# A dummy operand written by ScalarE, and half of one batch's transposes moved from TensorE to the DMA crossbar

## The chip, the cores and the metric

The kernel runs on one core of a Trainium2 chip. A core has TensorE (PE, matmuls), VectorE (DVE), ScalarE (ACT), GpSimd (POOL) and SyncE (SP), which here only issues DMAs; ScalarE can issue DMAs too. Each of these engines executes its instructions in the order in which the kernel writes them, and waits where an operand isn't there yet. 16 DMA engines move the data. The metric is device time in microseconds. The page gives the profiled execution's span, which is what its times are counted in.

## The reference

Two blocks, one after the other. The first is an attention without a square score matrix (8 batches, 8 heads, 576 positions, 64 per head); the second is a gated feed-forward block over all 4608 positions.

```
q_s = exp(q - max);  q_s = q_s / sum(q_s, over the 64 of a head)
k_s = exp(k - max);  k_s = k_s / sum(k_s, over the 576 positions)
kv  = einsum('bhsd,bhse->bhde', k_s, v)        # 64 x 64 per head
x   = einsum('bhsd,bhde->bhse', q_s, kv)       # -> 4608 x 512
g, val = x @ w_gate, x @ w_val                 # 512 -> 1536
out = (gelu(g) * val) @ w_out                  # 1536 -> 512
```

Input and output are float32; the kernel's matmuls take float16.

## The kernel before, in words

**Tiles.** The 576 positions of a batch lie over 128 partitions: a position is a multiple of nine plus n, and partition pairs hold the nine. Each partition has five columns n of 512 values (8 heads of 64). Column 0 is padding on the even partitions (for k -1e30, whose exp is 0) and the real remainder on the odd ones; columns 1 to 4 are the main part, 4 x 128 = 512 positions. The 64 remaining positions of all eight batches are gathered in one tile, `xtr`, and go through the feed-forward block as a ninth batch (`order` puts it before the last).

**Attention of a batch.** `exp` (L158, ScalarE) writes `eq` and `ek`, two buffers each, used by even and odd batches. `norm_sum` (L176, L178) sums a pair of heads on VectorE and takes the reciprocal; `norm_mul` (L195) multiplies `eq` by it, on VectorE or GpSimd. `cast_v` makes `v` float16. `unit_kv` (L222) multiplies k and v on TensorE for two pairs of heads, and `kv_norm` (L230, L233) scales and masks the result on VectorE into `kv_sb`. For the product with q, `eq` has to be transposed. Three ways are in use: `unit_t` (L305) does eight 128x128 transposes on TensorE for two pairs and copies them from PSUM (batches 0 and 1); `unit_td` (L323) has the DMA crossbar transpose a whole batch, 20 blocks, issued by SP (batches 2 to 7); `unit_trem` (L316) does that for column 0 alone (batches 0 and 1). `xq` and `xqr` pick the tile that a product reads. `unit_x` (L347) is the product of one pair, 128x512, and its copy into `xt`; `unit_xrem` (L363) is that of the remainder.

**Feed-forward of a batch.** For each of 12 blocks of 128 hidden columns, `ffn_fi` does four matmuls psg and four psv (L402); `gate` then has ScalarE take the gelu of psg (L407) and VectorE multiply it by psv (L409) into `ht`. Then for each of four columns n, 12 matmuls psy (L477) make the output rows, which VectorE or ScalarE copies from PSUM (`evac`, L524, L526) and SP stores (L487).

**Order.** The kernel is scheduled by hand. `plan` holds work that rides along: `at(b, kind, i, ...)` puts functions behind block i of batch b's feed-forward (FI) or behind column i of its output (NS; 10 + n or 14 + n lie in the middle of column n). Batch 1's attention rides on batch 0's last block (FI 11: its exps, the norms of pairs 0 to 2) and on its output columns: behind column 1 (NS 5) the transposes of pairs 0 and 1, in column 2 (NS 16) the kv of pairs 0 and 1 and the norm of pair 3, in column 3 (NS 17) the x of pairs 0 and 1. The rest of it lies in `first1`, which `ffn_first` calls between the first three blocks of batch 1: the transposes and kv of pairs 2 and 3 behind block 0, the x of pair 2 behind block 1, that of pair 3 behind block 2. `cut` says after how many of a column's 12 matmuls the middle lies.

**Start.** `warm_pe` runs dummy matmuls (L394) on a tile `warm` of zeros, before the first real work is there. VectorE writes `warm` after it has copied one value of q's first load (L548, L549), so the dummies begin when that load has landed. ScalarE's `preload` makes a one-element activation, to have its table loaded.

**PSUM.** `ps_big` has six banks, taken in turn under the tag "mm": batch 0's four psy, then x of pairs 0 and 1 of batch 1, then batch 1's psg and psv from the first psy's bank on. `ps_att` has two, for the attention's products.

Of the kernel before, what the change touches and what calls it, by code (L numbers as in the profile page):

```python
# [10 lines left out]
f16 = mybir.dt.float16  # L11
# [7 lines left out]
def kernel(  # L19
# [10 lines left out]
    nc = tc.nc  # L30

    B, H, S, D = q.shape
    C = H * D
    F = moe_w_gate.shape[1]
    P = 128
    HP = H // 2
    NFI = F // P
# [3 lines left out]
    NT = S // 64  # L41
    NM = 4
    NC = NM + 1
# [10 lines left out]
    att = ctx.enter_context(tc.tile_pool(name="att", bufs=2))  # L54
# [9 lines left out]
    warm = const.tile([P, 512], f16)  # L64
    ident = const.tile([P, P], f16)
    mask = const.tile([P, 2, D], f32)
    ones = const.tile([P, 1], f16)
    tiny = const.tile([P, 72], f32)
    ek_b, eq_b, v16_b = [], [], []
    for i in range(2):  # L70
# [4 lines left out]
    q0r = const.tile([64, H, D], f32)  # L75
    eq0r = const.tile([P, C], f16)
    ld_b = {nm: [const.tile([P, H, NC * D], f32, name=f"{nm}t{i}") for i in range(n)]
            for nm, n in (("k", 2), ("v", 1), ("q", 2))}
# [22 lines left out]
    QUAD = 2  # L101

    def heads(x, b, h0, h1):

        if b >= QUAD:
            return x.rearrange("p (t c) x -> p c t x", t=2)[:, h0 // 2:h1 // 2]
        return x[:, h0:h1]
# [24 lines left out]
    def copy_on(eng, dst, src):  # L132
        if eng == "pool":
            nc.gpsimd.tensor_copy(out=dst, in_=src)  # L134
        elif eng == "act":
            nc.scalar.copy(out=dst, in_=src)  # L136
        else:
            nc.vector.tensor_copy(out=dst, in_=src)  # L138
# [12 lines left out]
        copy_on(eng, wo_sb[:, 2 * c:2 * c + 2, :], wst[("wo", c)])  # L151


    def exp(nm, b, h0=0, h1=H, n0=0):
        dst = (ek_b if nm == "k" else eq_b)[b % 2]
        o, i = (("p n (c t d) -> p c t n d", "p c t (n d) -> p c t n d") if b >= QUAD else
                ("p n (h d) -> p h n d", "p h (n d) -> p h n d"))
        nc.scalar.activation(  # L158
            out=dst[:, n0:NC, h0 * D:h1 * D].rearrange(o, d=D, **({"t": 2} if b >= QUAD else {})),
            in_=heads(tiles[(nm, b)], b, h0, h1)[..., n0 * D:NC * D].rearrange(i, d=D),  # L160
            func=ACTF.Exp)

# [8 lines left out]

    def norm_sum(b, hp, n0=0):
        n = NC - n0
        e = eq_b[b % 2][:, n0:NC, hp * P:(hp + 1) * P].rearrange("p n (h d) -> p n h d", d=D)
        rq = att.tile([P, n, 2], f32, name="rq", tag="rq", bufs=4)
        nc.vector.reduce_sum(rq, e, axis=mybir.AxisListType.X)  # L176
        rrq = att.tile([P, n, 2], f32, name="rrq", tag="rrq", bufs=4)
        nc.vector.reciprocal(out=rrq, in_=rq)  # L178
        st[(b, "norm", hp)] = (e, rrq, n)

    def norm_pair(b, g, n0, engs):

        n = NC - n0
        e = eq_b[b % 2][:, n0:NC, 2 * g * P:(2 * g + 2) * P].rearrange("p n (h d) -> p n h d", d=D)
        rq = att.tile([P, n, 4], f32, name="rq2", tag="rq2", bufs=2)
        nc.vector.reduce_sum(rq, e, axis=mybir.AxisListType.X)
        rrq = att.tile([P, n, 4], f32, name="rrq2", tag="rrq2", bufs=2)
        nc.vector.reciprocal(out=rrq, in_=rq)
        for j, eng in enumerate(engs):
            st[(b, "norm", 2 * g + j)] = (e[:, :, 2 * j:2 * j + 2], rrq[:, :, 2 * j:2 * j + 2], n)  # L190
            norm_mul(b, 2 * g + j, eng)
# [23 lines left out]
    st = {}  # L215
# [74 lines left out]
    def get_eqt(b):  # L290
        if (b, "eqt") not in st:
            st[(b, "eqt")] = att.tile([P, NC * C], f16, name="eqt", tag="eqt")[
                :, 0:HP * MAIN].rearrange("p (h t) -> p h t", h=HP)
        return st[(b, "eqt")]

    def unit_t(b, g, eng="dve", between=()):
        eqt = get_eqt(b)
        pst = ps_att.tile([P, 2, MAIN], f16, name="pst", tag="att")
        st["evac_t"] = lambda eng: copy_on(eng, eqt[:, 2 * g:2 * g + 2, 0:MAIN], pst)
        for j in range(2):  # L300
            hp = 2 * g + j
            for f in between if j == 1 else ():
                f()
            for n in range(NM):
                nc.tensor.transpose(  # L305
                    pst[:, j, n * P:(n + 1) * P],
                    eq_b[b % 2][:, n + 1, hp * P:(hp + 1) * P], ident)
        if eng:
            st["evac_t"](eng)

    def unit_trem(b):

        src = eq0r[0:64] if b == 0 else eq_b[b % 2][:, 0, :]
        n = src.shape[0]
        t = att.tile([P, HP, n], f16, name=f"eqtr{b}", tag=f"eqtr{b}", bufs=1)
        nc.sync.dma_start_transpose(out=t, in_=src)  # L316
        st[(b, "eqtr")] = t[:, :, 0:n:n // REM]


    def unit_td(b):  # L320
# [3 lines left out]
                                    in_=eq_b[b % 2].rearrange("p n c -> p (n c)"))  # L324
        st[(b, "eqt4")] = t

    def xq(b, hp):

        if (b, "eqt4") in st:
            return st[(b, "eqt4")][:, 1:NC, hp]  # L330
        return st[(b, "eqt")][:, hp, 0:MAIN]

    def xqr(b, hp):
        if (b, "eqt4") in st:
            return st[(b, "eqt4")][:, 0, hp, 0:P:2]
        return st[(b, "eqtr")][:, hp, :]

    def get_xt(b):
# [52 lines left out]
    def warm_pe(n):  # L391
        ps = pswarm
        for _ in range(n):
            nc.tensor.matmul(ps, ident, warm, start=True, stop=True)  # L394

    def preload(func):
        nc.scalar.activation(out=tiny[:, 0:1], in_=tiny[:, 0:1], func=func)
# [146 lines left out]
    def load_batch(b, what=((q, "q"), (k, "k"), (v, "v"))):  # L544
        for src, nm in what:
            load(src, nm, b, 0, H, 0)

    nc.vector.tensor_copy(out=tiny[0:1, 1:2], in_=ld_b["q"][0][0:1, 0, D:D + 1])  # L548
    nc.vector.memset(warm, 0.0)  # L549
    preload(ACTF.Exp)  # L550
    exp("q", 0, 0, 4, 1)
    exp("q", 0, 4, 8, 1)
    exp("k", 0, 0, 4)
    exp("k", 0, 4, 8)
    norm_pair(0, 0, 1, ("dve", "pool"))
    warm_pe(13)
    unit_t(0, 0, None)
    evac_t0 = st["evac_t"]
    norm_pair(0, 1, 1, ("dve", "pool"))
# [20 lines left out]
        load(k, "k", 1, h0, h0 + 4, 0)  # L580
        load(v, "v", 1, h0, h0 + 4, 0)
    load_batch(2, ((q, "q"), (k, "k")))
    for h0 in (0, 4):
        nc.sync.dma_start(out=q0r[:, h0:h0 + 4], in_=q[0, h0:h0 + 4].rearrange(
            "h (m n) d -> m h (n d)", n=NT)[:, :, 0:D])
    cast_w("wg", 0, "pool")
    cast_w("wv", 0, "pool")
    for c in range(1, NW):
# [6 lines left out]
    FI, NS = 0, 1  # L595
    plan = {}

    def at(b, kind, i, *fns):
        plan.setdefault((b, kind, i), []).extend(fns)

    L = lambda f, *a: (lambda: f(*a))

    at(0, FI, NFI - 1, L(exp, "q", 1, 0, 4), L(exp, "q", 1, 4, 8), L(exp, "k", 1, 0, 4),
       L(cast_w_o, 3), L(cast_w_o, 4), L(cast_w_o, 5),
       L(norm, 1, 0), L(norm, 1, 1), L(norm_sum, 1, 2), L(norm_mul, 1, 2, "pool"),
       L(cast_v, 1, 0, 4, "act"), L(exp, "k", 1, 4, 8))
    at(0, NS, 5, L(unit_t, 1, 0))
    at(0, NS, 16, L(unit_kv, 1, 0), L(cast_v, 1, 4, 8), L(load_batch, 2, ((v, "v"),)),
       L(norm, 1, 3))
    at(0, NS, 17, L(unit_x, 1, 0, "act", True), L(unit_x, 1, 1, "act", True))  # L610
    at(0, NS, 7, L(preload, ACTF.Gelu))
    first1 = [[L(unit_t, 1, 1), L(unit_kv, 1, 1)], [L(unit_x, 1, 2, "act")],
              [L(unit_x, 1, 3, "dve")]]

    def x_upper0():
# [20 lines left out]
    for b in range(2, B):  # L636
# [3 lines left out]
        if b + 1 < B:  # L640
            n = b + 1
# [15 lines left out]
    for b in order:  # L657
        xt = get_xt(b) if b < B else xtr
        hts = []
        fi0 = 0  # L660
        if b < 2:
            hts = ffn_first0(xt, (x_upper0, L(unit_x, 0, 3, "dve"))) if b == 0 else ffn_first(xt, first1)
            fi0 = len(hts)
            ride(b, FI, fi0 - 1)
        for fi in range(fi0, NFI):
            hts.append(ffn_fi(xt, fi, b == 1 and fi == 7))
            ride(b, FI, fi)
        if b == 0:
            psys = []
            for ns in range(4):  # L670
                psys.append(ps_big.tile([P, C], f32, name="psy", tag="mm"))
                mm_out(psys[ns], hts, ns, range(0, NFI // 2))
                ride(b, NS, ns)
            for ns in range(4):
                cut = 9 if ns == 2 else 7 if ns == 3 else NFI
                mm_out(psys[ns], hts, ns, range(NFI // 2, cut))
                ride(b, NS, 14 + ns)
                mm_out(psys[ns], hts, ns, range(cut, NFI))
                evac(b, ns, psys[ns], "act" if ns == 3 else "dve")
                ride(b, NS, 4 + ns)  # L680
        else:
            for ns in range(4):
                if b == order[-1] and ns == 3:
                    last_rows(b, hts, ns)
                    break
                psy = ps_big.tile([P, C], f32, name="psy", tag="mm")
                mm_out(psy, hts, ns, range(NFI // 2))
                ride(b, NS, 10 + ns)
                mm_out(psy, hts, ns, range(NFI // 2, NFI))
                evac(b, ns, psy)  # L690
                ride(b, NS, ns)
# [30 lines left out]
```

## Time and profile before

| What | us |
| --- | --- |
| Median of 3 runs (lowest to highest) | 314.37 (314.08 to 315.01) |
| The profiled execution, its own time | 313.89 |
| Its span | 311.9 |
| TensorE matmuls busy | 301.3 |
| VectorE busy | 168.5 |
| ScalarE busy | 139.2 |
| GpSimd busy | 54.0 |
| First dummy matmul starts | 7.00 |
| Batch 1's first psg starts | 48.93 |
| Moved by DMA, and mean rate | 51.61 MB, 165 GB/s |

The page gives busy time by engine, then 40 slices of the span, where a digit is the busy share in tenths. The chain that ended last is followed back from the last instruction through what released each step; it dates a matmul by its place in the pipeline, some 0.15 us later than the timeline's start. In the timeline, a row is start, length, engine, line, operation and tiles; in square brackets stands the idle time before it and what ended it. SPq and ACTq are DMA issues of SP and ScalarE; PEld is TensorE's weight load. Matmuls overlap: a 128x512 one lasts 0.38 us and the next begins 0.216 us after it.

### The profile page before, as it was taken

What the parts mean: (1) busy time and instruction counts of PE and PEld (TensorE: products, weight loads), DVE (VectorE), ACT (ScalarE), POOL (GpSimd) and SP (SyncE); (2) the same over time, 40 slices, a digit from 0 to 9 for tenths busy, and PEclk for the clock granted to TensorE, in tenths of its full rate; (3) what the DMA queues carried; (4) which work ended last, traced back from release to release, by engine and by line L of the source; (5) the groups of instructions that cost most, each with busy time, mean ns of one, the idle gap of its engine ahead of it and who ended that gap; (6) DMA issues with size and microseconds to landing.
All of it is one profiled execution on the core that took longest, in us unless ns stands there. A gap on an engine that the chain in (4) does not pass through costs nothing.

```text
span 311.9 us, 4662 instructions
## 1 busy us (share of the span) xinstructions
PE 301.3 (97%) x1800; PEld 140.1 (45%) x1800; DVE 168.5 (54%) x293; ACT 139.2 (45%) x180; POOL 54.0 (17%) x67
## 2 busy tenths in 40 slices
PE   1999999999999999999999999999999999999995
PEld 0544455444445444444444444444444444444444
DVE  3944386484586478437853686358633443324331
ACT  3663475994843753366235643474330333013300
POOL 2657451071084000110003000300000000000000
PEclk9999999999999999999999999999999999999999
DMA  7999999609999017901593149412210200140002
GB/s 227 372 383 393 402 386 388 181 0 250 378 340 249 0 69 261 338 16 69 185 354 70 67 127 387 93 40 97 52 35 34 103 0 0 35 102 0 0 36 101
DMA packets 55189, 51.61 MB, mean 165 GB/s; under 512 B 18560, under 2 KB 50688, under 8 KB 55168
## 3 DMA queue, kind: packets, MB, share of 16 engines
q1 hardware_dynamic: 53440, 49.68, 49.2%
q10 hardware_dynamic: 1728, 1.64, 1.7%
q8 instruction: 14, 0.23, 0.3%
q14 instruction: 7, 0.06, 0.1%
HBM read 37.75 MB, written 9.44 MB: 151 GB/s over the span
## 4 chain that ended last, share of the span: by engine, by line
PE 96%; DMA 2%; DVE 1%; issue 0%; ACT 0%
PE psg L402 30%; PE psv L402 30%; PE psy L477 29%; DMA qt<-in_q_dram 2%; PE pswarm L394 2%; PE pskv L280 1%; PE psl L498 1%; PE psx L374 1%; PE psx L347 1%; PE pst L305 1%; PE pskv L222 0%; PE psxr L374 0%; PE pskv L258 0%; DVE eqt L138 0%; DVE v L138 0%; PE psx L356 0%
## 5 line engine op out<-in xcount | busy, mean ns | idle before, releaser
L407 ACT ACTIVATE gl<-psg 128x512 f32<-128x512 f32 x108 | 63.7, 598 | 122.7 <-PE psg L402 120.1
L409 DVE SCALAR_TENSOR_TENSOR ht<-psv,gl 128x512 f16<-128x512 f32 x108 | 74.1, 689 | 81.4 <-PE psv L402 76.8
L402 PE MATMUL psg<-xt,wg_sb 128*128 128x512 f16 x384 | 100.5, 379 | 0.0
L402 PE MATMUL psv<-xt,wv_sb 128*128 128x512 f16 x384 | 100.5, 379 | 0.0
L477 PE MATMUL psy<-wo_sb,ht 128*128 128x512 f16 x420 | 93.8, 379 | 0.0
L402 PEld LDWEIGHTS <-wv_sb 128*128 128x128 f16 x432 | 42.2, 98 | 50.8 <-issue 0.2
L402 PEld LDWEIGHTS <-wg_sb 128*128 128x128 f16 x432 | 42.1, 98 | 50.0
L477 PEld LDWEIGHTS <-ht 128*128 128x128 f16 x420 | 40.3, 98 | 48.2 <-issue 0.8
L526 DVE TENSOR_SCALAR yo<-psy 128x512 f32<-128x512 f32 x30 | 20.6, 688 | 33.5 <-PE psy L477 33.5
L134 POOL CAST v<-vt 128x640 f16<-128x640 f32 x26 | 18.2, 741 | 108.1 <-DMA vt<-in_v_dram 108.1
L176 DVE TENSOR_REDUCE rq<-eq 128x10 f32<-128x640 f16 x28 | 22.7, 812 | 5.1 <-ACT eq L158 4.7
L158 ACT ACTIVATE eq<-qt 128x2560 f16<-128x2560 f32 (+2 forms) x10 | 18.5, 1865 | 7.0 <-DMA qt<-in_q_dram 6.9
L158 ACT ACTIVATE ek<-kt 128x1280 f16<-128x1280 f32 (+1 forms) x11 | 19.1, 1749 | 4.4 <-DMA kt<-in_k_dram 4.4
L195 POOL TENSOR_TENSOR eq<-eq,rrq 128x640 f16<-128x640 f16 (+1 forms) x11 | 14.3, 1300 | 25.7 <-DVE rrq L178 17.6
L195 DVE TENSOR_TENSOR eq<-eq,rrq 128x640 f16<-128x640 f16 (+1 forms) x21 | 17.1, 813 | 0.2
L402 PE MATMUL psg<-xtr,wg_sb 128*128 128x512 f16 x48 | 12.3, 379 | 0.0
L402 PE MATMUL psv<-xtr,wv_sb 128*128 128x512 f16 x48 | 12.3, 379 | 0.0
L394 PE MATMUL pswarm<-warm,ident 128*128 128x512 f16 x15 | 5.4, 521 | 7.0 <-DVE warm L549 7.0
L138 DVE CAST xt<-psx 128x512 f16<-128x512 f32 (+1 forms) x17 | 10.7, 667 | 1.9 <-PE psx L347 1.8
L158 ACT ACT_TABLE_LOAD x8 | 10.3, 1283 | 0.6 <-DMA qt<-in_q_dram 0.4
L136 ACT CAST xt<-psx 128x512 f16<-128x512 f32 (+1 forms) x16 | 8.6, 575 | 2.9 <-PE psx L347 2.3
L136 ACT CAST xtr<-psxr 128x128 f16<-128x128 f32 (+1 forms) x6 | 1.7, 283 | 17.8 <-PE psxr L374 17.8
(68 smaller groups left out, 109.0 us busy)
## 6 DMA issues: line engine op xcount, KB each, us to landing
out_dram<-yo SPq DMA_DIRECT2D x12, 512.0 KB, 3.5
kt<-in_k_dram SPq DMA_DIRECT2D x7, 640.0 KB, 7.0
vt<-in_v_dram SPq DMA_DIRECT2D x7, 640.0 KB, 8.6
qt<-in_q_dram SPq DMA_DIRECT2D x7, 640.0 KB, 5.6
qt<-in_q_dram SPq DMA_DIRECT2D x8, 512.0 KB, 6.0
wost<-in_moe_w_out_dram SPq DMA_DIRECT2D x6, 512.0 KB, 7.9
kt<-in_k_dram SPq DMA_DIRECT2D x6, 512.0 KB, 7.5
vt<-in_v_dram SPq DMA_DIRECT2D x6, 512.0 KB, 9.0
```

Of the source, the lines that this page charges most:

```text
L134: nc.gpsimd.tensor_copy(out=dst, in_=src)
L136: nc.scalar.copy(out=dst, in_=src)
L138: nc.vector.tensor_copy(out=dst, in_=src)
L158: nc.scalar.activation(out=dst[:, n0:NC, h0 * D:h1 * D].rearrange(o, d=D, **({"t": 2} if b >= QUAD else {})), in_=heads(tiles[(nm, b)], b, ...
L176: nc.vector.reduce_sum(rq, e, axis=mybir.AxisListType.X)
L195: (nc.gpsimd if eng == "pool" else nc.vector).tensor_tensor(out=e, in0=e, in1=rrq.unsqueeze(-1).to_broadcast((P, n, 2, D)), op=ALU.mult)
L394: nc.tensor.matmul(ps, ident, warm, start=True, stop=True)
L402: nc.tensor.matmul(ps, w[:, ci, fi * P:(fi + 1) * P], xt[:, ci, :], start=(ci == 0), stop=(ci == HP - 1))
L407: nc.scalar.activation(out=gl, in_=psg, func=ACTF.Gelu)
L409: nc.vector.scalar_tensor_tensor(out=ht, in0=psv, scalar=_H_SCALE, in1=gl, op0=ALU.mult, op1=ALU.mult)
L477: nc.tensor.matmul(psy, hts[fi][:, ns * P:(ns + 1) * P], wo_sb[:, fi, :], start=(fi == 0), stop=(fi == NFI - 1))
L526: nc.vector.tensor_scalar(out=yo, in0=psy, scalar1=1.0 / _H_SCALE, scalar2=None, op0=ALU.mult)
```

## The change

- `warm` is written by ScalarE, by a copy of one zero broadcast to 128x512, behind the preload of the exp table. VectorE's one-value copy and its memset are gone. 12 dummy matmuls instead of 13 stand before the first transposes.
- The `eq` of batch 1 gets another layout, in two halves of four heads, so that the upper half (pairs 2 and 3) is one contiguous run of five columns of 256 values in each partition. `e_q` gives the view for `exp`, the norms and the transposes.
- The eight TensorE transposes of batch 1's pairs 2 and 3, and their copy by VectorE, are gone. `unit_td1` has the crossbar transpose the upper half instead, ten blocks, with a DMA that ScalarE issues between the x of pair 0 and the x of pair 1 (NS 17). It covers column 0 too, so `unit_trem` of batch 1 does the lower half alone, two blocks instead of four.
- The norm of pair 3 moves from NS 16 to FI 11, behind that of pair 2, and GpSimd multiplies it instead of VectorE.
- The copy of x of pair 1 moves from ScalarE to VectorE.
- In column 3, the middle lies behind 9 matmuls instead of 7.
- `q0r`, the remainder of batch 0's q, is loaded by one DMA instead of two.

```diff
+    def e_q(b, n0, h0, h1):
+        if b != 1:
+            return eq_b[b % 2][:, n0:NC, h0 * D:h1 * D]
+        g = h0 // 4
+        return eq_b[1].rearrange("p n c -> p (n c)").rearrange("p (g n c) -> p g n c", g=2, n=NC)[
+            :, g, n0:NC, (h0 - 4 * g) * D:(h1 - 4 * g) * D]
...
     def unit_trem(b):
-        src = eq0r[0:64] if b == 0 else eq_b[b % 2][:, 0, :]
+        src = eq0r[0:64] if b == 0 else e_q(1, 0, 0, 4)[:, 0, :]
         n = src.shape[0]
-        t = att.tile([P, HP, n], f16, name=f"eqtr{b}", tag=f"eqtr{b}", bufs=1)
+        t = att.tile([P, HP if b == 0 else 2, n], f16, name=f"eqtr{b}", tag=f"eqtr{b}", bufs=1)
...
+    def unit_td1():
+        t = att.tile([P, NC, 2, P], f16, name="eqt1", tag="eqt1", bufs=1)
+        nc.scalar.dma_start_transpose(
+            out=t.rearrange("p n j t -> p (n j) t"),
+            in_=eq_b[1].rearrange("p n c -> p (n c)")[:, NC * C // 2:])
+        st["eqt1"] = t
     def xq(b, hp):
...
+        if b == 1 and hp >= 2:
+            return st["eqt1"][:, 1:NC, hp - 2]
...
-    nc.vector.tensor_copy(out=tiny[0:1, 1:2], in_=ld_b["q"][0][0:1, 0, D:D + 1])
-    nc.vector.memset(warm, 0.0)
     preload(ACTF.Exp)
+    nc.scalar.copy(out=warm, in_=tiny[:, 1:2].to_broadcast((P, 512)))
...
-    warm_pe(13)
+    warm_pe(12)
...
-    for h0 in (0, 4):
-        nc.sync.dma_start(out=q0r[:, h0:h0 + 4], in_=q[0, h0:h0 + 4].rearrange(
-            "h (m n) d -> m h (n d)", n=NT)[:, :, 0:D])
+    nc.sync.dma_start(out=q0r, in_=q[0].rearrange("h (m n) d -> m h (n d)", n=NT)[:, :, 0:D])
...
        L(norm, 1, 0), L(norm, 1, 1), L(norm_sum, 1, 2), L(norm_mul, 1, 2, "pool"),
+       L(norm_sum, 1, 3), L(norm_mul, 1, 3, "pool"),
        L(cast_v, 1, 0, 4, "act"), L(exp, "k", 1, 4, 8))
     at(0, NS, 5, L(unit_t, 1, 0))
-    at(0, NS, 16, L(unit_kv, 1, 0), L(cast_v, 1, 4, 8), L(load_batch, 2, ((v, "v"),)),
-       L(norm, 1, 3))
-    at(0, NS, 17, L(unit_x, 1, 0, "act", True), L(unit_x, 1, 1, "act", True))
+    at(0, NS, 16, L(unit_kv, 1, 0), L(cast_v, 1, 4, 8), L(load_batch, 2, ((v, "v"),)))
+    at(0, NS, 17, L(unit_x, 1, 0, "act", True), L(unit_td1), L(unit_x, 1, 1, "dve", True))
     at(0, NS, 7, L(preload, ACTF.Gelu))
-    first1 = [[L(unit_t, 1, 1), L(unit_kv, 1, 1)], [L(unit_x, 1, 2, "act")],
+    first1 = [[L(unit_kv, 1, 1)], [L(unit_x, 1, 2, "act")],
               [L(unit_x, 1, 3, "dve")]]
...
-                cut = 9 if ns == 2 else 7 if ns == 3 else NFI
+                cut = 9 if ns == 2 else 9 if ns == 3 else NFI
```

More of the change, by code (lines that the diff above doesn't have):

```diff
@@ L151, in cast_w_o @@
         copy_on(eng, wo_sb[:, 2 * c:2 * c + 2, :], wst[("wo", c)])
+    def e_q(b, n0, h0, h1):
[4 more added lines that the diff above has]
+            :, g, n0:NC, (h0 - 4 * g) * D:(h1 - 4 * g) * D]
     def exp(nm, b, h0=0, h1=H, n0=0):
-        dst = (ek_b if nm == "k" else eq_b)[b % 2]
+        dst = ek_b[b % 2][:, n0:NC, h0 * D:h1 * D] if nm == "k" else e_q(b, n0, h0, h1)
         o, i = (("p n (c t d) -> p c t n d", "p c t (n d) -> p c t n d") if b >= QUAD else
@@ L158, in exp @@
         nc.scalar.activation(
-            out=dst[:, n0:NC, h0 * D:h1 * D].rearrange(o, d=D, **({"t": 2} if b >= QUAD else {})),
+            out=dst.rearrange(o, d=D, **({"t": 2} if b >= QUAD else {})),
             in_=heads(tiles[(nm, b)], b, h0, h1)[..., n0 * D:NC * D].rearrange(i, d=D),
@@ L173, in norm_sum @@
         n = NC - n0
-        e = eq_b[b % 2][:, n0:NC, hp * P:(hp + 1) * P].rearrange("p n (h d) -> p n h d", d=D)
+        e = e_q(b, n0, 2 * hp, 2 * hp + 2).rearrange("p n (h d) -> p n h d", d=D)
         rq = att.tile([P, n, 2], f32, name="rq", tag="rq", bufs=4)
@@ L306, in unit_t @@
                     pst[:, j, n * P:(n + 1) * P],
-                    eq_b[b % 2][:, n + 1, hp * P:(hp + 1) * P], ident)
+                    e_q(b, 0, 2 * hp, 2 * hp + 2)[:, n + 1], ident)
         if eng:
@@ L335, in xqr @@
             return st[(b, "eqt4")][:, 0, hp, 0:P:2]
+        if b == 1 and hp >= 2:
+            return st["eqt1"][:, 0, hp - 2, 0:P:2]
         return st[(b, "eqtr")][:, hp, :]
```

## The prediction

> **What bounds the kernel now.** I read the page's busy shares and slices first, then the chain that ended last, then the timeline of each engine around the places that the diff touches, then the DMA queues.
>
> ```profile
> PE 301.3 (97%) x1800; PEld 140.1 (45%) x1800; DVE 168.5 (54%) x293; ACT 139.2 (45%) x180; POOL 54.0 (17%) x67
> ...
> PE   1999999999999999999999999999999999999995
> ...
> DMA  7999999609999017901593149412210200140002
> ```
>
> TensorE is full from 7 us to the end and the chain is 96% TensorE, so a removed matmul is worth its spacing (0.216 us for 512 columns, four of psg in 0.86 us) only while nothing else is late. In the chain, the eight transposes that the change takes out of batch 1 hold 0.45 us:
>
> ```profile
> 49.95 0.45 PE pst L305 x8
> ```
>
>
> The timeline between batch 0's last matmuls and batch 1's first (start, length):
>
> ```profile
> 45.90 0.68 DVE L138 COPY eqt<-pst 128x1024 f16<-128x1024 f16 x1
> ...
> 46.75 0.17 DVE L230 RECIPROCAL rck<-pskv 128x2 f32<-128x2 f32 x1 [0.17 <-PE pskv L222]
> 46.95 0.61 DVE L233 SCALAR_TENSOR_TENSOR kv_sb<-pskv,rck,mask 128x128 f16<-128x128 f32 x2
> 47.36 0.10 PEld L347 LDWEIGHTS <-kv_sb 128*128 128x128 f16 x1 [0.28 <-DVE kv_sb L233]
> 47.41 0.60 PE L347 MATMUL psx<-eqt,kv_sb 128*128 128x512 f16 x2
> ...
> 47.83 1.07 ACT L136 CAST xt<-psx 128x512 f16<-128x512 f32 x2 [0.62 <-PE psx L347]
> ...
> 49.13 0.60 ACT L524 ACTIVATE yo<-psy 128x512 f32<-128x512 f32 x1 [0.23 <-PE psy L477]
> 49.74 1.28 ACT L397 ACT_TABLE_LOAD   x1
> ...
> 51.68 0.38 PE L347 MATMUL psx<-eqt,kv_sb 128*128 128x512 f16 x1
> ...
> 52.90 1.38 SPq L316 DMA_TRANSPOSE eqtr<-eq  x1
> ```
>
> See two things. VectorE works from 40.09 us with one gap (0.17 us before rck), and its kv_sb comes just as TensorE wants it: no slack. And batch 1's third psx (heads 4 and 5) starts at 51.68 us, only 4.3 us after the first.
>
> The transfers, first two slices of 1 us, whose last two columns are DMA share and GB/s: the one in question, and one in which a whole 20-block crossbar transpose (issued at 223.12 us by SP, 3.10 us of issue) has the engines to itself. Then the queues between 8 and 10 us, when both carried loads (packets, MB, share):
>
> ```profile
> 51.00:52.00 1.00, 1.00 (x6) 0.42 (x5) 0.82 (x4) 0.23 (x2) 0.00 (x0) 1.00 1.18 365
> ...
> 225.00:226.00 1.00, 1.00 (x6) 0.44 (x5) 0.69 (x1) 0.20 (x1) 0.00 (x0) 1.00 1.14 214
> ```
>
> ```profile
> q1 hardware_dynamic: 352, 0.43, 58.2%
> q10 hardware_dynamic: 353, 0.35, 48.9%
> ```
>
> At 51 us the engines are saturated with loads, and they stay so until about 57.7 us; the transpose of 223 us had them alone.
>
> **What the Trainium skill says.** "DMA: Bandwidth & Descriptors", section "Queues, rings and completion order": each DMA engine takes turns between the queues at packet granularity. The trace agrees: 353 packets of ScalarE's queue against 352 of SP's. The same page, "Silent corruption: two transposing streams in flight at once": a transpose on one queue has to wait until one on another queue has landed; no run here shows it, but SP's eqtr will have to wait for ScalarE's transpose. "TensorE: Matmul & The Clock Gate", "Part 1: The HAM clock gate": half clock until about 3.4 us of work, and again after an idle window of that length. The trace agrees on the first: dummy matmuls are 0.43 us apart until 10.75 us, 3.75 us after their start, and 0.216 us after.
>
> **The change part by part.**
>
> *Start.* ScalarE's copy follows its preload (ends 4.35 us) and costs 0.58 us (the 128x512 cast, 575 ns), in an idle stretch: its first exp starts at 6.60. The dummies start near 5.0 instead of 7.00 and, twelve at no more than 0.43 us, end by 10.2; now the transposes behind them start at 11.61.
>
> ```profile
> 9.36 1.48 POOL L195 TENSOR_TENSOR eq<-eq,rrq 128x512 f16<-128x512 f16 x1 [6.76 <-DVE rrq L188]
> ...
> 11.38 0.69 DVE L195 TENSOR_TENSOR eq<-eq,rrq 128x512 f16<-128x512 f16 x1
> ...
> 12.26 0.69 DVE L138 COPY eqt<-pst 128x1024 f16<-128x1024 f16 x1 [0.19 <-PE pst L305]
> ```
>
> They need GpSimd's product (10.84), so they can start at about 10.9, but the copy behind them on VectorE waits for VectorE's own product until 12.07. Gain: 12.26 - 12.07 = 0.19 us, not the 0.7 of the transposes. VectorE's removed copy and memset (0.41 us) lay before an exp that it waits for anyway.
>
> *SP.* Two loads of q0r (2.20 us of issue) become one, perhaps 1 us shorter. Behind them is a store that waits for VectorE; q0r is read past 70 us. Nothing. eqtr, now two blocks, must wait for the new transpose and starts some 1.3 us later than 52.90; it landed 7.2 us after issue and psxr reads it at 65.92, which leaves over 4 us. The next SP transpose, at 69.09, is beyond it.
>
> *GpSimd.* One more product of 1.26 us, after the one at 44.98 to 46.24: it ends at 47.5, as the casts of v behind it (47.52, waiting for their load) begin. Nothing, and without that gap at most 1.26 us on the casts that batch 1's second kv needs at 50.24.
>
> *VectorE.* Sum and reciprocal of pair 3 move ahead of the two yo copies: 44.76 - 43.78 = 0.98 us. The gap of 0.15 to 0.17 us takes a part, so kv_sb, and with it psx, can start at 47.41 + 0.98 - 0.15 = 48.24. TensorE, with two matmuls put ahead (0.43), would be there at 47.84, at 47.65 with the start's gain. So it stalls 0.4 to 0.6 us: 0.4 late, and the start's 0.19 is lost, since VectorE's stretch hangs on the load of q that ScalarE waits for at 37.49. What the change removes later on VectorE (product 1.00 us, copy of pst 0.69) is off the chain; the second psx cast, 0.69, moves there into that room.
>
> *The crossbar transpose.* ScalarE reaches its issue at the cast of the first psx: 48.24 + 0.42 = 48.66, or after the cast, 49.25; I take 49.0. Alone, the 20 blocks (655 KB) began to move 1.25 us after issue, moved for 3.02 us at about 217 GB/s and landed 0.63 us later (4.9 in all). Ten blocks alone: 1.25 + 1.51 + 0.63 = 3.39 us, landing at 52.4. That is the low bound. Under load, packet for packet: 80 packets of 256 B on each engine at 18.9 ns (217/16 GB/s), each behind a load's 1 KB at 42 ns (390/16 GB/s), 4.9 us: landing at 55.8. The high bound. I take the middle, 54.1, because nothing shows whether turns are taken for single 256-byte rows or for groups of them.
>
> *Behind that issue on ScalarE.* It holds ScalarE for about 2.0 us (1.38 for 4 blocks, 3.10 for 20). Then yo (0.60) ends near 51.7, the Gelu table at 53.0, its dummy at 53.2, against 51.24 now. yo frees the bank for psv of the second column block, which TensorE reaches near 51.2: a stall of some 0.5 us, inside the wait for the transpose. The cast of the third psx can start at 53.2 or later.
>
> *Sum.* The third psx moves from 51.68 to 54.1 + 0.1 = 54.2: +2.5 us. Inside it are the 0.45 of the transposes and the 0.19 of the start, gained and lost. Everything behind it on TensorE keeps its order and has no slack to give back, so the span goes from 311.9 to 314.4, the profiled execution from 313.89 to 316.4, and the median of the runs, 0.48 above it, from 314.37 to 316.9.
>
> **The rivals.** *The queue and the bank, not the landing.* The transpose lands near 52.4 in spite of the loads; then ScalarE's 2 us of issue set the third psx (near 52.5) and its cast at 53.2, which TensorE needs 1.3 us after psx: +0.8 to +1.1, 315.3. For it: the separate ring. Against: the slice at 51 us is saturated.
>
> *The clock falls.* The stalls between 51 and 54 us, some 2.5 us, make TensorE lose its clock; 3.4 us at half clock cost 1.7 more: 318.6. For it: the page's window. Against: the idle time is shorter than that window. The same price would come from dummies that end by 10.2, before the real work.
>
> *Not slower.* The transpose lands by 51.5, 2.5 us after issue, before TensorE asks. Then what is left is -0.45 for the transposes and +0.4 for kv_sb: 314.3; with kv_sb in time as well, -0.45 - 0.19, 313.7. For it: a small eqtr, 64 partitions, landed in 2.4 us on idle engines. Against: it had a fifth of this one's bytes and no loads beside it. It decides at a landing of 2.7 us or less.
>
> **How the numbers follow.** Chances: late landing 0.57, queue and bank 0.21, clock 0.12, not slower 0.10. The predicted time is the first's, 316.9; its own range is 316.0 to 318.5. Down to 315.2 takes in the second rival, up to 319.2 a landing at 55.8 or most of the clock's loss; the last rival and the far tail stay out. 0.3% is 0.94 us, about what runs spread over 314.08 to 315.01 can tell. Faster needs the last rival with kv_sb in time: 0.03. Same: the rest of it and the low edge of the second, 0.12. Slower 0.85.
>
> **What would show it.** Dummies from 5 us and the eqt copy at 12.07; the first batch-1 psx near 48.2, waiting for kv_sb; a transpose on ScalarE's queue of some 2 us from about 49.0, landing about 5 us later; the third psx waiting on that DMA until about 54; the same distances from there to the end. Wrong if the third psx starts before 52, if ScalarE issues the transpose earlier than the first psx cast, or if psg is spaced 0.43 us anywhere behind 16 us.

## The result, and the profile after

The changed kernel takes 324.20 us (median of 4 runs, 323.51 to 324.83) where the kernel before takes 314.62 (its table above has 314.37, of three runs): a ratio of 1.0305, interval 1.0275 to 1.0336. It is 9.6 us slower. The direction was forecast, the size was not: the forecast was 316.9, and the range ended at 319.2. The profiled execution's span is 322.3 us against 311.9, that is 10.4 us longer, and nearly all of it comes in between 51 and 64 us.

The page of the kernel after. TensorE has a hole in its seventh and eighth slice (48 to 64 us), and its clock falls there:

```profile
PE   3899994599999999999999999999999999999995
...
PEclk9999998599999999999999999999999999999999
```

The chain that ended last, which before was TensorE almost alone, now runs through GpSimd's product of pair 3, a cast of v, and then for 11.3 us through the new transpose:

```profile
44.97 2.46 POOL eq L203 x2
...
47.52 0.98 POOL v L134 x2
48.50 11.29 DMA eqt<-eq
...
59.93 0.59 PE psx L367
60.52 0.85 PE psg L422 x2
```

The step from the cast of v to the transpose is an inference of this view. The timeline shows what the issue stood behind on ScalarE, the start of its cast of the first product at 48.44.

The timeline of the same stretch; line 367 is now `unit_x`, 338 is `unit_td1`, 422 is the feed-forward's matmul:

```profile
46.81 0.68 DVE L138 COPY eqt<-pst 128x1024 f16<-128x1024 f16 x1
47.41 0.16 DVE L238 RECIPROCAL rck<-pskv 128x2 f32<-128x2 f32 x1
...
48.01 0.10 PEld L367 LDWEIGHTS <-kv_sb 128*128 128x128 f16 x1 [0.59 <-DVE kv_sb L241]
48.02 0.65 PE L367 MATMUL psx<-eqt,kv_sb 128*128 128x512 f16 x2
...
48.44 0.59 ACT L136 CAST xt<-psx 128x512 f16<-128x512 f32 x1 [1.25 <-PE psx L367]
...
48.50 1.90 ACTq L338 DMA_TRANSPOSE eqt<-eq  x1
...
50.45 0.60 ACT L544 ACTIVATE yo<-psy 128x512 f32<-128x512 f32 x1 [1.42 <-issue]
...
51.02 0.59 PE L422 MATMUL psv<-xt,wv_sb 128*128 128x512 f16 x2
...
59.93 0.59 PE L367 MATMUL psx<-eqt,kv_sb 128*128 128x512 f16 x1 [8.32 <-DMA eqt<-eq]
...
60.31 1.06 PE L422 MATMUL psg<-xt,wg_sb 128*128 128x512 f16 x2
...
60.50 1.41 SPq L324 DMA_TRANSPOSE eqtr<-eq  x1
```

The first product starts at 48.02 and ScalarE issues the transpose at 48.50, both close to the forecast. The third product, at 51.68 before, starts at 59.93: 8.25 us later, after a wait of 8.32. Two psg then take 1.06 us instead of 0.59, since the clock is at half. It is whole again at about 64 us. In stretches of 4 us, with the granted clock, DMA share (of packets that overlap, so that it can pass 1) and GB/s in the last three columns, the changed kernel:

```profile
54.00:58.00 4.00, 0.00 (x0) 0.00 (x0) 0.00 (x0) 0.00 (x0) 0.00 (x0) 0.50 1.06 242
58.00:62.00 4.00, 2.07 (x5) 0.74 (x6) 0.00 (x0) 0.59 (x1) 0.00 (x0) 0.50 0.95 287
62.00:66.00 4.00, 4.00 (x15) 1.66 (x14) 1.04 (x2) 0.98 (x3) 0.00 (x0) 0.73 0.21 60
```

The kernel before in the first of them:

```profile
54.00:58.00 4.00, 4.00 (x20) 1.83 (x19) 2.33 (x4) 2.93 (x5) 0.00 (x0) 1.00 1.17 381
```

It moved 381 GB/s between 54 and 58 us; the changed one moves 242 with its DMA engines nearly as busy (1.06 against 1.17).

### The profile page after: what moved, and what is told of

Its sections match the earlier page's. It is cut to its first block, busy times and chain, and to the rows that moved or that the text cites. A ratio compares the mean times of both kernels' runs of the same rounds, so it can differ in the third digit from the quotient of the medians.

```text
span 322.3 us, 4645 instructions
## 1 busy us (share of the span) xinstructions
PE 303.7 (94%) x1791; PEld 140.2 (44%) x1791; DVE 166.7 (52%) x290; ACT 139.2 (43%) x180; POOL 55.2 (17%) x68
## 4 chain that ended last, share of the span: by engine, by line
PE 80%; DMA 13%; POOL 2%; DVE 1%; SPq 1%; ACT 1%; issue 0%; ACTq 0%; POOLq 0%
PE psg L422 26%; PE psv L422 26%; PE psy L497 25%; DMA wgst<-in_moe_w_gate_dram 5%; DMA qt<-in_q_dram 5%; DMA eqt<-eq 4%; PE pskv L288 1%; SPq L128 1%; PE psl L518 1%; PE psx L394 1%; POOL eq L203 1%; DVE rq L184 1%; POOL wg_sb L134 1%; DVE eq L203 1%; ACT L166 0%; ACT eq L166 0%
## 5 line engine op out<-in xcount | busy, mean ns | idle before, releaser
L422 PEld LDWEIGHTS <-wv_sb 128*128 128x128 f16 x432 | 42.4, 98 | 51.5 <-issue 1.6
L203 POOL TENSOR_TENSOR eq<-eq,rrq 128x640 f16<-128x640 f16 (+1 forms) x12 | 15.5, 1296 | 36.4 <-DVE rrq L186 28.3
L138 DVE CAST xt<-psx 128x512 f16<-128x512 f32 (+1 forms) x18 | 11.3, 666 | 11.7 <-PE psx L367 11.6
L203 DVE TENSOR_TENSOR eq<-eq,rrq 128x640 f16<-128x640 f16 (+1 forms) x20 | 16.1, 803 | 0.1
L136 ACT CAST xt<-psx 128x512 f16<-128x512 f32 (+1 forms) x15 | 8.1, 574 | 10.3 <-PE psx L367 10.1
L367 PE MATMUL psx<-eqt,kv_sb 128*128 128x512 f16 x7 | 3.0, 450 | 8.4 <-DMA eqt<-eq 8.3
L166 ACT ACT_TABLE_LOAD x8 | 10.3, 1283 | 0.7 <-DMA qt<-in_q_dram 0.5
```

The lines of the kernel that those rows point to most:

```text
L166: nc.scalar.activation(out=dst.rearrange(o, d=D, **({"t": 2} if b >= QUAD else {})), in_=heads(tiles[(nm, b)], b, h0, h1)[..., n0 * D:NC * ...
L203: (nc.gpsimd if eng == "pool" else nc.vector).tensor_tensor(out=e, in0=e, in1=rrq.unsqueeze(-1).to_broadcast((P, n, 2, D)), op=ALU.mult)
L422: nc.tensor.matmul(ps, w[:, ci, fi * P:(fi + 1) * P], xt[:, ci, :], start=(ci == 0), stop=(ci == HP - 1))
```

## The experiments

Each edit is against the changed kernel unless it says otherwise. "Third product" is batch 1's product of pair 2, which reads the new transpose (in e1 TensorE's own). "First packet" is the first packet of the DMA in the trace's packet records; in e3 it can't be told from SP's others.

| Run | Issued | First packet | Landed | Third product | Span | Median |
| --- | --- | --- | --- | --- | --- | --- |
| before | - | - | - | 51.68 | 311.9 | 314.62 |
| changed | 48.50 | 51.72 | 59.79 | 59.93 | 322.3 | 324.20 |
| e1 own transposes kept | 48.28 | 51.54 | 59.1 | 51.67 | 311.9 | 314.32 |
| e2 quiet engines | 49.23 | 51.26 | 54.5 | 54.69 | 315.0 | 318.00 |
| e3 on SP's queue | 49.16 | - | 56.3 | 56.38 | 318.3 | 320.37 |
| e4 dummies in the wait | 48.33 | 51.66 | 59.3 | 59.38 | 319.6 | 321.74 |
| e5 v later | 48.38 | 51.68 | 58.7 | 58.80 | 320.9 | 322.06 |
| e6 store later | 48.56 | 51.83 | 58.5 | 58.57 | 320.3 | 322.39 |
| e7 quiet from 49 | 48.61 | 49.90 | 52.2 | 52.33 | 312.6 | 314.66 |
| e9 plain copy | 49.57 | 52.94 | 59.4 | 59.47 | 322.5 | 324.78 |
| e10 products later | 48.14 | 49.43 | 51.8 | 51.98 | 312.0 | 314.65 |
| e12 plain copy, long rows | 48.50 | 51.60 | 54.3 | 54.43 | 314.7 | 317.65 |

The experiments' medians belong to runs of the kernel before of 313.7 to 314.3. Some medians hide executions with a lower granted clock; e10 and e11 come back to this.

### The wait, or the traffic itself (e1)

```diff
     def xq(b, hp):
...
-        if b == 1 and hp >= 2:
-            return st["eqt1"][:, 1:NC, hp - 2]
...
-    first1 = [[L(unit_kv, 1, 1)], [L(unit_x, 1, 2, "act")],
+    first1 = [[L(unit_t, 1, 1), L(unit_kv, 1, 1)], [L(unit_x, 1, 2, "act")],
```

> The changed kernel, but TensorE's eight transposes and their copy are back and the third and fourth product read them; ScalarE's crossbar transpose is still issued, and only the remainder product, 14 us later, reads its column 0. Theory (the wait for the landing is the loss, the transfer's slowness harms nobody else): no wait at the third product, TensorE's clock stays whole, the landing still 10 to 12 us after issue, time 314.5 to 316. Rival (the slowed loads or ScalarE's occupied queue cost as much by themselves): 318 or more, with a wait elsewhere.

It took 314.32 us, 1.0031 of the kernel before (1.0006 to 1.0056), with the same span. Beside the same slow transpose, TensorE doesn't notice:

```profile
48.28 1.94 ACTq L338 DMA_TRANSPOSE eqt<-eq  x1
...
51.67 0.38 PE L365 MATMUL psx<-eqt,kv_sb 128*128 128x512 f16 x1
...
59.77 1.39 SPq L324 DMA_TRANSPOSE eqtr<-eq  x1
```

So the loss is the wait for the landing and what the wait does to TensorE. The slowed loads of batch 2 and ScalarE's 1.9 us of issue cost nothing that this profiled execution shows; the interval of the medians leaves up to 1.8 us. Four of the twelve executions, with a mean granted clock of 0.992 to 0.995, took 316.4 to 316.9 us; where they lost it isn't traced.

### The clock's part (e4)

```diff
         psx = (ps_big if big else ps_att).tile([P, MAIN], f32, name="psx",
                                                tag="mm" if big else "att")
+        for _ in range(36 if (b, hp) == (1, 2) else 0):
+            nc.tensor.matmul(psx, ident, warm, start=True, stop=True)
```

> The changed kernel, with 36 dummy matmuls (7.8 us at full clock) into the bank of the third product ahead of it, so that TensorE works while it waits. If the landing stays where it is (59.8) and the rest of the loss is TensorE's half clock from 60 to 64 us: 2.0 us faster than the changed kernel, 322.2, psg spaced 0.216 behind the third product. If the half clock costs nothing that isn't lost anyway: no change, 324.2.

```profile
51.27 7.93 PE L368 MATMUL psx<-warm,ident 128*128 128x512 f16 x36
59.38 0.38 PE L369 MATMUL psx<-eqt,kv_sb 128*128 128x512 f16 x1 [0.18 <-DMA eqt<-eq]
59.60 0.59 PE L424 MATMUL psg<-xt,wg_sb 128*128 128x512 f16 x2
```

The two psg behind the product are back at 0.59 us. Here the third product is 59.38 - 51.68 = 7.70 us late, and the span 319.6 - 311.9 = 7.7 us longer: nothing else is lost. In the changed kernel 8.25 of 10.4 us are the delay, so 2.15 us are the half clock. That fits the timeline: from 59.93 to about 64.15 TensorE works 4.2 us at half pace, which loses 2.1. (321.74 is 0.5 below what was expected because this landing came 0.5 us earlier.)

### Quiet engines (e2, then e7)

In e2, SP's store of batch 0's first two columns, the load of batch 2's v and that of q0r are issued behind batch 1's eqtr, which waits for the transpose anyway. In e7, batch 2's k is too; the diff is that of e7, and e2 leaves its first two lines and loads v alone at the end. `late_store` is the store that `evac` would have issued.

```diff
-    load_batch(2, ((q, "q"), (k, "k")))
+    load_batch(2, ((q, "q"),))
-    nc.sync.dma_start(out=q0r, in_=q[0].rearrange("h (m n) d -> m h (n d)", n=NT)[:, :, 0:D])
+    load_q0r = lambda: nc.sync.dma_start(out=q0r, in_=q[0].rearrange("h (m n) d -> m h (n d)", n=NT)[:, :, 0:D])
...
-    at(0, NS, 16, L(unit_kv, 1, 0), L(cast_v, 1, 4, 8), L(load_batch, 2, ((v, "v"),)))
+    at(0, NS, 16, L(unit_kv, 1, 0), L(cast_v, 1, 4, 8))
-    at(1, FI, 2, L(unit_trem, 1))
+    at(1, FI, 2, L(unit_trem, 1), lambda: st["late_store"](),
+       L(load_batch, 2, ((k, "k"), (v, "v"))), load_q0r)
```

> The changed kernel, but SP's store of batch 0's first columns, its loads of batch 2's v and of q0r are issued behind batch 1's eqtr, after the crossbar transpose has landed, so that it finds only the end of k's load on the engines. Theory (the transpose is slow because it shares the engines with SP's transfers): landing 3.4 to 4.5 us after issue, third product at 52 to 53, clock whole, time 315 to 316.5. Rival (ScalarE's queue or this form of transpose is slow by itself): landing 8 us or more after issue, time 321 or more.

> The kernel with the quiet engines, and the load of batch 2's k too is issued behind batch 1's eqtr, so that nothing but q is on the engines, and that only until about 49. If the transpose alone takes what half of a 20-block one takes on idle engines: landing 3.2 to 3.8 us after issue, third product near 52.2, time 314.8 to 316. If ten blocks on ScalarE's queue cost 5 us even so: time 317 or more.

The quiet engines of e2:

```profile
49.23 1.65 ACTq L338 DMA_TRANSPOSE eqt<-eq  x1
...
54.69 0.38 PE L367 MATMUL psx<-eqt,kv_sb 128*128 128x512 f16 x1 [2.36 <-DMA eqt<-eq]
```

The kernel that is quiet from 49 us, e7:

```profile
48.61 1.46 ACTq L338 DMA_TRANSPOSE eqt<-eq  x1
...
52.33 0.38 PE L367 MATMUL psx<-eqt,kv_sb 128*128 128x512 f16 x1 [0.61 <-DMA eqt<-eq]
```

e7 is the clearest case: landing 3.6 us after issue, 314.66 us, 1.0023 of the kernel before (1.0007 to 1.0039). ScalarE's queue and this form of transpose are not slow by themselves. e2 misses its range on both counts: beside the end of k's load alone, which stays on the engines until 52.8, the landing takes 5.3 us, and the time is 318.0.

### Which partner (e5, e6)

e5 moves the load of v alone behind eqtr (the diff below), e6 the store of columns 0 and 1 alone, as `late_store`.

```diff
-    at(0, NS, 16, L(unit_kv, 1, 0), L(cast_v, 1, 4, 8), L(load_batch, 2, ((v, "v"),)))
+    at(0, NS, 16, L(unit_kv, 1, 0), L(cast_v, 1, 4, 8))
...
-    at(1, FI, 2, L(unit_trem, 1))
+    at(1, FI, 2, L(unit_trem, 1), L(load_batch, 2, ((v, "v"),)))
```

> The changed kernel, but the load of batch 2's v is issued behind batch 1's eqtr, after the crossbar transpose has landed; q0r and the store of batch 0's first columns stay in front of it. Theory (the store is the partner that slows it, as both move from SBUF at once between 52 and 55 us): still 7 to 9 us from issue to landing, third product at 55.5 to 57.5, time 319 to 322. Rival (the load of v is the partner): landing 5.5 us or less after issue, as on the quiet engines, time 316.5 to 318.5.

> The changed kernel, but the store of batch 0's first columns is issued behind batch 1's eqtr; q0r and the load of v stay. Theory (the store is the partner): landing 5 to 6.5 us after issue, third product at 53.5 to 55, time 317 to 319. Rival (the load of v is the partner, or any transfer is): landing 8 us or more after issue, time 321 or more.

Landing 10.3 and 9.9 us after issue, 322.06 and 322.39 us: either transfer is enough, and the theory that named the store falls. e5 is less clean than meant: without v in front of it, the store of columns 2 and 3 was issued at once, so that two stores lay beside the transpose. e6 is nearly clean: its other store was issued at 51.11, but moved only 11 of its 128 packets before the transpose was through.

### One queue instead of two (e3)

```diff
-        nc.scalar.dma_start_transpose(
+        nc.sync.dma_start_transpose(
...
-       L(cast_v, 1, 4, 8), L(load_batch, 2, ((v, "v"),)))
+       L(cast_v, 1, 4, 8), L(unit_td1), L(load_batch, 2, ((v, "v"),)))
```

> The changed kernel, but SP issues the ten-block transpose, behind the store of batch 0's first columns and ahead of the load of v. Theory (what hurts is the packet-by-packet mixture of two queues): in one queue it starts when k, q0r and the store are through, moves at some 200 GB/s, lands 7 to 8.5 us after 47.6, that is at 54.5 to 56; third product there, time 317.5 to 320. Rival (a transpose is slow beside any queued transfer, whatever the queue): landing at 59 or later, time 323 or more.

```profile
49.16 3.88 SPq L338 DMA_TRANSPOSE eqt<-eq  x1
...
56.38 0.38 PE L367 MATMUL psx<-eqt,kv_sb 128*128 128x512 f16 x1 [3.98 <-DMA eqt<-eq]
```

320.37 us, just outside what was expected, for the landing came 7.1 us after an issue that began 1.5 us later than I had set it. In one queue the transpose goes behind the store and ahead of v, and lands 3.5 us earlier than in the changed kernel, though issued later.

### The crossbar, or any small rows (e9, e12)

Both replace the transpose by a plain copy of the same 327 KB, and so leave the transposition out: the third and fourth product, and the remainder's, read untransposed values. In e9 the rows have 256 bytes, as the transpose's packets, in e12 2560. The diff is that of e12; in e9 the tile has ten rows of P + 16 values, of which P are written.

```diff
-        nc.scalar.dma_start_transpose(
-            out=t.rearrange("p n j t -> p (n j) t"),
-            in_=eq_b[1].rearrange("p n c -> p (n c)")[:, NC * C // 2:])
+        nc.scalar.dma_start(
+            out=t.rearrange("p n j t -> p (n j t)"),
+            in_=eq_b[1].rearrange("p n c -> p (n c)")[:, NC * C // 2:])
```

> The changed kernel, but ScalarE's DMA copies the ten blocks, in 256-byte rows and within each partition, and does not transpose them; the third and fourth product read the untransposed values. Everything else, the queue, the moment and SP's transfers beside it, is as in the changed kernel. Theory (the crossbar is what doesn't go with other transfers): the copy's first byte still waits for the transfers issued before it, but it lands within 7 us of its issue, and the rate of all DMA between 52 and 58 us stays above 330 GB/s; third product before 55.7, time 320 or less. Rival (any small-row transfer of a second queue slows like this): landing 10 us or more after issue, 200 to 250 GB/s in that stretch, time 323 or more.

> As the plain copy, but each partition's 2560 bytes are one row, so that each DMA engine has some 8 to 24 packets of it instead of 80; again nothing is transposed, and the products read untransposed values. Theory (the queues take turns packet by packet, so the number of packets sets the time): the first byte comes as late, 3 to 3.5 us after issue, and the copy is through 1 to 1.5 us after it, landing 4.5 to 6 us after issue, third product at 54 to 55.5, time 317 to 319. Rival (the bytes, or the loads queued on the engines, set it): landing 8 us or more after issue, time 321 or more.

The DMA totals between 52 and 58 us, first the kernel before, then the changed kernel:

```profile
DMA packets 1909, 2.31 MB, mean 385 GB/s; under 512 B 602, under 2 KB 1678, under 8 KB 1909
DMA packets 1858, 1.33 MB, mean 221 GB/s; under 512 B 1361, under 2 KB 1730, under 8 KB 1857
```

The plain copy in 256-byte rows, e9, and its third product:

```profile
DMA packets 2638, 2.06 MB, mean 343 GB/s; under 512 B 1468, under 2 KB 2518, under 8 KB 2637
```

```profile
59.47 0.59 PE L368 MATMUL psx<-eqt,kv_sb 128*128 128x512 f16 x1 [6.80 <-DMA eqt<-eq]
```

The plain copy in long rows, e12, and its third product:

```profile
DMA packets 1553, 2.40 MB, mean 400 GB/s; under 512 B 182, under 2 KB 1228, under 8 KB 1552
```

```profile
54.43 0.38 PE L367 MATMUL psx<-eqt,kv_sb 128*128 128x512 f16 x1 [2.81 <-DMA eqt<-eq]
```

e9 splits the two theories. The copy lands 9.8 us after issue, so the crossbar is not needed for a late landing; but the engines keep 343 GB/s, and with the crossbar only 221. That its time (324.78) equals the transpose's is in part chance: in the profiled execution the clock fell at the start too (shown further down), which put the first product and with it the issue 1.06 us later than in the changed kernel, and the half clock behind the wait lasted until 65.1 us. e12 lands 5.8 us after issue: its packets, counted with the 16 small ones that close it, are 144 instead of 1296, for the same bytes, and they move in 2.2 us (51.60 to 53.76) instead of 6.0 (52.94 to 58.97). So beside a loaded queue the same bytes took nearly three times as long in small rows.

### The smaller parts (e8, e10, e11)

e8 makes the move of pair 3's norm in the kernel before, with pair 1's copy on VectorE and `cut` 9.

```diff
        L(norm_sum, 1, 2), L(norm_mul, 1, 2, "pool"),
+       L(norm_sum, 1, 3), L(norm_mul, 1, 3, "pool"),
...
-       L(norm, 1, 3))
-    at(0, NS, 17, L(unit_x, 1, 0, "act", True), L(unit_x, 1, 1, "act", True))
+    at(0, NS, 17, L(unit_x, 1, 0, "act", True), L(unit_x, 1, 1, "dve", True))
```

> The kernel before, with the norm of pair 3 ahead of batch 0's yo copies and multiplied by GpSimd, the x of pair 1 copied by VectorE, and the middle of column 3 behind 9 matmuls, as in the change; TensorE's transposes, the dummies and q0r as before. Expected from the prediction's VectorE step: the first product of batch 1 is 0.3 to 0.5 us later than two matmuls behind its old place, so +0.3 to +0.5 us on 314; if VectorE's extra 0.98 us is hidden: no change.

314.55 us, 1.0022 (1.0008 to 1.0035): between 0.25 and 1.1 us slower, the size expected. The profiled execution shows no stall (first product at 47.91), because ScalarE got q 0.3 us earlier in it; so the place of the loss isn't shown here. In the changed kernel's own trace it is: six psy from 46.46, 0.216 us apart, would let the product start at 47.75; it starts at 48.02.

e10 takes the quiet kernel e7 and puts the third product between psg and psv of the third block, the fourth behind that psv; `ffn_first` calls the first of the two functions ahead of psv.

```diff
-    first1 = [[L(unit_kv, 1, 1)], [L(unit_x, 1, 2, "act")],
-              [L(unit_x, 1, 3, "dve")]]
+    first1 = [[L(unit_kv, 1, 1)], [],
+              [L(unit_x, 1, 2, "act"), L(unit_x, 1, 3, "dve")]]
```

> The kernel that is quiet from 49 us, with the third product of batch 1 between psg and psv of the third block and the fourth behind that psv, 0.43 us of TensorE work later. Expected: the wait of 0.61 us for the landing falls to about 0.2, time 0.3 to 0.4 us below that kernel, 314.2 to 314.5, no measurable difference from the kernel before. If the wait only moves to the cast behind it: as that kernel, 314.7.

The wait fell from 0.61 to 0.33 us, but the median didn't: 314.65, 1.0022 (1.0010 to 1.0033). It lies between two groups. Eleven of the 20 executions, with a mean granted clock of 0.999 or 1, took 314.07 to 314.77, in the median 314.31; nine, with 0.995, took 315.1 to 315.7. e7's six with 0.998 or more have a median of 314.64. Sorted so, which was done afterwards, the step gave about the 0.3 us expected, and with the traffic out of the way and the clock whole this version is level with the kernel before. Where the nine lost their clock isn't traced.

e11 makes the start alone in the kernel before: ScalarE's copy, 12 dummies, one load of q0r, as in the diff of the change.

> The kernel before, with ScalarE writing the dummy operand, 12 dummies and one load of q0r, as in the change, and nothing else. Expected from the prediction's start step: TensorE's real work begins up to 0.19 us earlier, no measurable difference (0.0 to -0.2 us). If the dummies' early end costs TensorE its clock: 1.5 us or more slower.

314.11 us, 1.0004 (0.9990 to 1.0018): no difference in the middle, but one at the end. Five of the 22 executions have a mean granted clock of 0.995 or 0.987 and spans of 312.7 to 314.6 us; the other seventeen have 0.998 or more and 311.5 to 311.9. The kernel before never went below 0.998, in 43 executions, nor did e8 with the old start, in 14. So the second expectation, a loss of clock, came true in about a quarter of the executions, with 1 to 3 us. None of these versions beats the kernel before by what a measurement can tell.

## Why the prediction was wrong

**The start was right in its times, not in its clock.** In the changed kernel ScalarE's copy takes 0.60 us from 4.84, and the transposes don't wait for dummies any more but for GpSimd:

```profile
4.84 0.60 ACT L569 CAST warm<-tiny 128x512 f16<-128x512 f32 x1
5.49 4.75 PE L414 MATMUL pswarm<-warm,ident 128*128 128x512 f16 x12 [5.49 <-ACT warm L569]
...
10.99 0.40 PE L313 MATMUL pst<-ident,eq 128*128 128x128 f16 x4 [0.43 <-POOL eq L203]
...
12.09 0.68 DVE L138 COPY eqt<-pst 128x1024 f16<-128x1024 f16 x1
```

The copy to eqt starts at 12.09 (12.07 forecast, 12.26 before). About 0.1 us of it is left at batch 0's first psy (37.02 against 37.11), which e11 can't resolve.

In this execution the clock held: it is whole in every stretch from 10 to 50 us, so the start has no part in the 10.4 us. But e11 shows that it does not always hold, and the profiled executions of e3 and e9, which have the same start, show where it goes. This is e9, with the clock third from the end of the first line:

```profile
14.00:16.00 2.00, 2.00 (x25) 1.18 (x20) 1.64 (x5) 0.96 (x3) 1.54 (x4) 0.50 1.13 366
...
12.68 0.40 PE L253 MATMUL pks<-ones,ek 128*128 128x1 f16 x10 [0.58 <-ACT ek L166]
...
16.36 0.63 PE L423 MATMUL psv<-xt,wv_sb 128*128 128x512 f16 x1
16.79 0.63 PE L423 MATMUL psg<-xt,wg_sb 128*128 128x512 f16 x1
```

The dummies end near 10.2 us, what follows comes in pieces, and the clock is at half from 13.9 to 17.3 us (13.3 to 16.8 in e3). The first product of batch 1 then starts 1.06 us later than in the changed kernel, in e3 0.84. The prediction named this cause, "dummies that end by 10.2, before the real work", but only inside the rival of the clock; its own sum gave the start 0.19 us of gain and no such loss, and psg 0.43 us apart behind 16 us was one of its signs of being wrong.

**SP, GpSimd and VectorE were right.** GpSimd's two products end at 47.45 and its casts start at 47.52, as before. The first product starts at 48.02, forecast 48.24; the stall is 0.27 us (forecast 0.4 to 0.6): the yo copies start 0.91 us later (45.67 against 44.76), not 0.98, and the gap before rck took 0.25 of it, not 0.15, so that rck starts at 47.41 instead of 46.75. The one load of q0r cost nothing.

**ScalarE's issue was right.** 1.90 us, forecast 2.0. It begins at 48.50, 0.06 us after the cast's start: my low choice of 48.66 was nearer than the 49.0 I took. yo ended at 51.05, and psv of the second block (51.02) did not have to wait for its bank, so the rival of queue and bank had no place.

**The step that failed is "the crossbar transpose".** It gave a landing of 52.4 to 55.8 and took 54.1; it was 59.8. By its own terms:

- From issue to the first byte: 1.25 us taken, from a transpose on idle engines; 3.22 measured (48.50 to 51.72). In e7 it was 1.29. In the other runs with k and q0r ahead of it on SP it was 3.3 whatever came behind (e1, e4, e5, e6), and 3.4 and 3.1 for the plain copies of e9 and e12; with the end of k's load alone ahead (e2) it was 2.0. I had let another queue's backlog slow the moving but not the start.
- The moving: 1.51 us alone, 4.9 at most, with one turn per packet; 7.5 measured (51.72 to 59.19), and 1.7 on the quiet engines of e7. The number of packets does weigh: e9, the same rows without the crossbar, took 6.0, and e12 with a ninth of the packets 2.2. What the upper bound had wrong is how long a packet lasts. Packets, MB and share of 16 engines of SP's queue (q1) and ScalarE's (q10) while the transfer moved, first in the changed kernel, then in e9:

```profile
q1 hardware_dynamic: 1122, 1.34, 79.4%
q10 hardware_dynamic: 1311, 0.33, 36.2%
...
q1 hardware_dynamic: 1199, 1.39, 63.3%
q10 hardware_dynamic: 1295, 0.33, 24.0%
```

  Divided by the packets, these shares are 85 ns for one of SP's and 33 ns for one of the transpose's, where the bound took 42 and 18.9; in e9 they are 51 and 18. So even without the crossbar SP's packets are longer than a 1 KB load (those of the store take 159 ns in the kernel before), and beside it everything slows: between 53 and 54 us of the changed kernel three of the store's 24 packets last over 1 us. The turns themselves are not shown to be one for one: in e9 ScalarE's queue moved 565 packets against SP's 145 between 53 and 54 us, and 88 against 342 between 56 and 57.
- The tail: 0.63 taken, 0.6 measured.

Against the forecast of 54.1 that is 5.7 us more. Taking the middle of the two bounds was no safer than the bounds were, and the high one wasn't one.

**The clock** was a rival at 0.12, priced at 1.7 us. Its loss came with the long wait and cost 2.15. In the profiled executions a wait of 3.98 us (e3) was enough to lose it, waits of 2.36 (e2) and 2.81 us (e12) were not; the "Trainium skill", on its page "TensorE: Matmul & The Clock Gate", "Part 1: The HAM clock gate", sets the idle window at about 3.4 us, which lies between. One idle stretch of that length isn't needed, though: behind the dummies of e3 and e9 TensorE never waits longer than 0.76 us before the clock falls, and there the measurement differs from the page.

**The sum's form was right.** Everything behind the third product kept its order and had no slack: with the clock kept, e4's delay and its span agree within 0.1 us. What made this time wrong is the delay put into the sum. And the rival "not slower" would have needed a landing by 51.5; even e7's 3.6 us lands at 52.2.

**What stays open.** Why the rate of all transfers falls so far beside the crossbar is not shown: the runs show that it does, from 385 to 221 GB/s, that a plain copy in equal rows leaves 343, and that single packets of both kinds then last up to 1 us and more. What the first byte waits for isn't shown either. It isn't the end of everything issued earlier: by the packet records about 160 of q0r's 512 packets had started before it in the changed kernel, about 440 in e9. Nor is it shown why the start keeps its clock in some executions and loses it in others.

## What to carry to other kernels

Cost a transfer that something waits for in the stage where it will run: read the DMA share there, what is queued ahead of it on every queue, and its number of packets besides its bytes. A transpose on the crossbar that takes 3.6 us on quiet engines took 11.3 between a store and two loads, and it is free only where nobody needs it for that long. If a bound is to carry the far end of a range, let it hold the start, the turns and the slowest packets together. And where a change touches what keeps TensorE busy, look at the granted clock of every execution: a loss in one of four leaves the median where it was.

## What the runs showed that I had not expected

- A DMA on ScalarE's queue moved its first byte later with transfers queued before it on SP's: 3.1 to 3.4 us after issue behind k and q0r, 2.0 behind the end of k alone, 1.3 on quiet engines. A plain copy was as late as a transpose.
- Ten transposed blocks beside plain transfers brought all DMA from 385 GB/s (the kernel before, 52 to 58 us) to 221; a plain copy in equally small rows left 343, in long rows 400.
- TensorE's clock can fall after the wait is over: in e3 the third product starts at 56.38 and the first matmuls behind it keep the full pace, and only from about 57.7 are psg and psv 0.43 us apart, until 61. The same half clock of 3.4 us appears at the start of e3 and e9, behind work with no long wait in it.
